# A list scheduler for everything behind the attention in an attention and two-expert-layer kernel

## The chip, the cores and the metric

The kernel runs on one core of a Trainium2 chip. The metric is the time of one execution on the device in microseconds (us); lower is better. A core has TensorE (PE: matmuls; PEld: its weight loads), VectorE (DVE), ScalarE (ACT) and GpSimd (POOL); SP issues most DMA. Each engine works through a queue of its own, in the order in which the program was written, and waits on semaphores for the others.

## The reference

```python
q_bits = (einsum('bhsd,dk->bhsk', q, proj) > 0)          # the same for k; 6 bits make a bucket
mask = q_bucket[..., :, None] == k_bucket[..., None, :]
attn = softmax(where(mask, q @ k.T / 8, -1e9)) @ v       # q, k, v: (2, 8, 768, 64)
x = attn.transpose(0, 2, 1, 3).reshape(1536, 512)
h = maximum(maximum(x @ w1, x @ w2), x @ w3)             # 512 -> 768
x = h @ w_out                                            # 768 -> 512
h = x @ w_in                                             # 512 -> 2048
g = where(h >= 1, h, where(h <= -1, 0, (h + 1) ** 2 / 4))
out = g @ w_out2                                         # 2048 -> 512
```

q, k, v and proj come as 32-bit floats, the layers' weights as 64-bit ones; the output is 32-bit.

## The kernel before

The attention works through the 16 heads (functions in `attention`); its order on every engine comes from an older planner, `Work`, and is the same in both kernels. It ends with the normalisation of the last pair of heads: `pair_recip`, the fold of two halves (L576, L580), a broadcast of the reciprocals by DMA (`rb<-d`, L605), `norm_mult` (L614), `norm_hi` and `norm_lo` (L623, L627). The first matmuls of the first expert layer are written in among these (the generator `mlp_steps`).

Everything behind it is `mlp`. Tokens lie in three tiles of 512 columns (`tok(c)`); every matrix product is made from three matmuls of a high and a low part (`mm3`, L308). Four products follow each other: the first layer (18 weights, the maximum of three kept in `h`), the second (`b<-hh`, 8 weights of 384 columns), the third with the activation `g` (`l3`, `g_out`), and the fourth, which adds into `acc` (`l4`, L1235, L1242). From the fifth weight of the first layer on, and in the third, weights are taken in pairs: `pair_units` makes four blocks of output from seven block products in place of eight. It needs four sums of the pair's weights (`s`, from `sr`, L245 to L250), three difference tiles of the input (`x_d`, from `raw`, L1027, L1104, L1020, L1023) and, on the way, copies of one PSUM bank into another, which seed it: among them the sum `d` (L1072), which VectorE writes from the bank `b` and `x7`. The next product into `b`, `product(b, "s1", T1, False)`, can't start before VectorE has read it. A pair is eleven units of six matmuls.

A weight is read as 64-bit words (`wr`), and has a front of one ScalarE and four VectorE steps (L211, L213, L218, L222, L226), which make a 32-bit value (`wg`), and a back of a ScalarE cast (L234, the high part) and a GpSimd subtraction (L268, the low part). Two tiles of raw words and seven of finished weights exist.

What sets the order is the program text: `w_tick(2)` after each unit takes the weights' work on by two steps, whichever weight is next; `flush` writes the split of the last result one result later; banks go around in the order in which they come free in the text. There are no costs and no due times behind the attention.

Of the kernel before, what the change touches and what calls it, by code (L numbers as in the profile page):

```python
# [111 lines left out]

@with_exitstack
def lsh_attention_moe_kernel(
# [85 lines left out]
    def w_steps(n):  # L200
# [11 lines left out]
        yield  # L212
# [3 lines left out]
        yield  # L216
        g2 = w_p.tile([128, 512], I32, tag="wg2", name="wg2", bufs=2)[:, 0:cols]
# [3 lines left out]
        yield  # L221
# [3 lines left out]
        yield  # L225
# [3 lines left out]
        yield  # L229
        if n % WBUFS < WEARLY:  # L230
            w = w_p.tile([128, 2, 512], F32R, tag="w", name="w", bufs=WEARLY)
        else:
            w = w_state["more"].tile([128, 2, 512], F32R, tag="wx", name="wx", bufs=WBUFS - WEARLY)
        nc.scalar.copy(out=w[:, 0, 0:cols], in_=f32(g2))  # L234
        splits[n] = w
        low_todo.append((n, w, g2, cols))
        g2s[n] = f32(g2)
        if n not in pair_at:
            return
        yield  # L240
        a1, a2 = g2s.pop(n - 1), g2s.pop(n)
# [1079 lines left out]
```

## Time and profile before

| | us |
|---|---|
| three timed runs | 673.18, 673.73, 677.01 |
| median | 673.73 |
| the profiled execution's own time | 671.09 |
| its span, first to last instruction | 669.3 |
| DVE busy in the span | 495.6 |
| ACT busy in the span | 396.6 |
| POOL busy in the span | 352.8 |

A share of busy time is a mean over stages with different limits; the rows below are therefore cut by stage. PE and DVE in the rows are TensorE and VectorE, L and a number is a line of the kernel, and `b<-x_hl,wx` reads: writes tile b, reads x_hl and wx. `PEclk` is the share of full clock that TensorE was granted (0.5 is 1.2 GHz, 1.0 is 2.4 GHz).

### The profile page before, as it was taken

What the parts mean: (1) busy time and instruction counts of PE and PEld (TensorE: products, weight loads), DVE (VectorE), ACT (ScalarE), POOL (GpSimd) and SP (SyncE); (2) the same over time, 40 slices, a digit from 0 to 9 for tenths busy, and PEclk for the clock granted to TensorE, in tenths of its full rate; (3) what the DMA queues carried; (4) which work ended last, traced back from release to release, by engine and by line L of the source; (5) the groups of instructions that cost most, each with busy time, mean ns of one, the idle gap of its engine ahead of it and who ended that gap; (6) DMA issues with size and microseconds to landing.
All of it is one profiled execution on the core that took longest, in us unless ns stands there. A gap on an engine that the chain in (4) does not pass through costs nothing.

```text
span 669.3 us, 11587 instructions
## 1 busy us (share of the span) xinstructions
PE 645.2 (96%) x4323; PEld 513.4 (77%) x4323; DVE 495.6 (74%) x803; ACT 396.6 (59%) x740; POOL 352.8 (53%) x313
## 2 busy tenths in 40 slices
PE   7999999999999899889999998799999999999998
PEld 5668777778867677768888886588888888888886
DVE  5788989999863899878844477655786969696554
ACT  7687877887782344555443246778748374646440
POOL 6437547766322577657645255754646464645340
PEclk8999999999999989999999999899999999999999
DMA  6857787786333012231211211221211212121004
GB/s 189 224 122 185 198 213 182 199 247 153 92 112 81 32 64 95 94 95 55 71 49 47 64 63 59 68 94 64 64 63 64 89 37 94 36 92 63 1 0 189
DMA packets 27857, 66.99 MB, mean 100 GB/s; under 512 B 4165, under 2 KB 9125, under 8 KB 27801
## 3 DMA queue, kind: packets, MB, share of 16 engines
q1 hardware_dynamic: 27488, 66.21, 33.9%
q8 instruction: 34, 0.56, 0.3%
q14 instruction: 23, 0.18, 0.1%
q10 hardware_dynamic: 312, 0.04, 0.0%
HBM read 46.17 MB, written 3.19 MB: 74 GB/s over the span
## 4 chain that ended last, share of the span: by engine, by line
PE 79%; DVE 12%; ACT 4%; issue 3%; DMA 1%; POOL 1%; DVEq 0%; ACTq 0%; SPq 0%; POOLq 0%
PE b L308 24%; PE b L1235 18%; PE u_ps L308 7%; PE s_ps L449 6%; PE t_ps L482 5%; PE u_ps L543 5%; PE s_ps L452 5%; PE u_ps L510 3%; DVE raw L1027 2%; PE u_ps L1235 2%; PE pj_ps L425 2%; DVE pj_ps L213 1%; DVE wg L226 1%; DVE wg L218 1%; DVE pj_ps L222 1%
## 5 line engine op out<-in xcount | busy, mean ns | idle before, releaser
L459 DVE TENSOR_SCALAR_CACHE_REDUCE p<-s_ps 128x768 f32<-128x768 f32 x96 | 89.7, 951 | 13.3 <-PE s_ps L452 10.0
L474 ACT ACTIVATE p<-p,nm 128x768 f32<-128x768 f32 x96 | 89.7, 936 | 7.2 <-DVE p L459 6.7
L1213 POOL TENSOR_TENSOR g<-r,g 128x512 fp32r<-128x512 f32 x48 | 62.7, 1306 | 37.9 <-ACT g L1212 37.7
L449 PE MATMUL s_ps<-lo,q 128*128 128x384 f32 x192 | 72.5, 378 | 3.1 <-POOL lo L416 2.0
L308 PE MATMUL b<-x_d,s 128*128 128x512 f32 x270 | 68.6, 398 | 6.4 <-DVE u_ps L1072 2.6
L1235 PE MATMUL b<-wx,g 128*128 128x512 f32 x264 | 67.5, 393 | 4.5 <-ACT wx L234 3.3
L308 PE MATMUL b<-x_hl,wx 128*128 128x512 f32 x264 | 65.7, 393 | 1.5 <-ACT x_hl L1163 1.2
L308 PEld LDWEIGHTS b<-x_d,s 128*128 128x128 f32 x270 | 51.2, 192 | 19.6 <-DVE u_ps L1072 3.4
L452 PE MATMUL s_ps<-hi,q 76*128 76x384 f32 x192 | 66.1, 344 | 0.0
L213 DVE SCALAR_TENSOR_TENSOR pj_ps<-pj_ps,wr 128x512 f32<-128x512 f32 (+1 forms) x55 | 37.2, 677 | 37.5 <-ACT pj_ps L211 37.5
L1235 PE MATMUL b<-w,g 128*128 128x512 f32 (+1 forms) x264 | 64.6, 384 | 0.0
L234 ACT CAST wx<-wg 128x512 fp32r<-128x512 f32 (+1 forms) x32 | 19.4, 605 | 73.3 <-DVE wg L226 73.3
L1235 PEld LDWEIGHTS b<-wx,g 128*128 128x128 f32 x264 | 49.8, 189 | 15.7 <-ACT wx L234 3.7
L268 POOL TENSOR_TENSOR wx<-wg,wx 128x512 fp32r<-128x512 f32 (+1 forms) x32 | 40.7, 1273 | 39.3 <-ACT wx L234 36.1
L308 PEld LDWEIGHTS b<-x_hl,wx 128*128 128x128 f32 x264 | 50.1, 190 | 12.7 <-ACT x_hl L1163 1.7
L308 PE MATMUL b<-x_hl,w 128*128 128x512 f32 (+1 forms) x282 | 59.5, 363 | 0.0
L1242 DVE TENSOR_TENSOR acc<-b,acc 128x512 f32<-128x512 f32 (+1 forms) x77 | 51.6, 677 | 8.9 <-PE b L1235 8.9
L1235 PEld LDWEIGHTS b<-w,g 128*128 128x128 f32 x264 | 48.9, 188 | 9.9
L308 PEld LDWEIGHTS b<-x_hl,w 128*128 128x128 f32 x282 | 48.0, 189 | 8.8 <-issue 0.6
L449 PEld LDWEIGHTS s_ps<-lo,q 128*128 128x128 f32 x192 | 36.7, 191 | 21.3 <-DVE p L459 8.6
L492 ACT COPY pt<-t_ps 128x768 f32<-128x768 f32 (+1 forms) x59 | 41.0, 706 | 17.0 <-PE t_ps L482 14.7
L268 POOL TENSOR_TENSOR w<-wg,w 128x512 fp32r<-128x512 f32 (+1 forms) x26 | 33.0, 1269 | 29.9 <-ACT w L234 26.8
(154 smaller groups left out, 1495.9 us busy)
## 6 DMA issues: line engine op xcount, KB each, us to landing
wr<-in_w SPq DMA_DIRECT2D x48, 512.0 KB
r<-in_kq SPq DMA_DIRECT2D x15, 384.0 KB
q<-hi SPq DMA_DIRECT2D x15, 384.0 KB
v<-in_v SPq DMA_DIRECT2D x21, 256.0 KB
rb<-d SPq DMA_DIRECT2D x16, 192.0 KB
wr<-in_w SPq DMA_DIRECT2D x8, 384.0 KB
q<-lo SPq DMA_DIRECT2D x15, 192.0 KB
lo<-hi SPq DMA_DIRECT2D x15, 192.0 KB
```

Source lines behind the costliest of these rows:

```text
L213: nc.vector.scalar_tensor_tensor(out=f32(g), in0=f32(g), scalar=TINY_SQ, in1=f32(high), op0=ALU.is_ge, op1=ALU.mult)
L268: nc.gpsimd.tensor_tensor(out=w[:, 1, 0:cols], in0=f32(g2), in1=f32(w[:, 0, 0:cols]), op=ALU.subtract)
L308: nc.tensor.matmul(out=outp, lhsT=w_[a], rhs=x_[b_], start=(begins and i == 0 and jj == 0), stop=(ends and i == n - 1 and jj == 2), skip_g ...
L449: nc.tensor.matmul(out=o, lhsT=hd["qa"][:, qs], rhs=hd["lo"][:, ks], start=True, stop=False)
L452: nc.tensor.matmul(out=o, lhsT=hd["qb"][0:76, qs], rhs=hd["hi"][0:76, ks], start=False, stop=True)
L459: nc.vector.tensor_scalar(out=p.rearrange("p (a k) -> p a k", a=2), in0=s_ps[bank.at][:, :, 0:HALF], scalar1=MASKED, scalar2=MASKED, op0=A ...
L474: nc.scalar.activation(out=p, in_=p, func=ACTF.Exp, scale=-1.0, bias=tl[n]["nm"], accum_out=sums_of(h // 2)[:, c:c + 1],)
L482: nc.tensor.transpose(out=t_ps[:, half, j * 128:(j + 1) * 128], in_=tl[n]["p"][:, kt * 128:(kt + 1) * 128], identity=ident,)
L492: copy(out=grp[g][:, 3 * a:3 * b_, r * 128:(r + 1) * 128].rearrange("p (a j) q -> p a j q", a=b_ - a), in_=t_ps[:, a:b_, 0:HALF].rearrange ...
L1213: nc.gpsimd.tensor_tensor(out=lo, in0=r, in1=f32(hi), op=ALU.subtract)
L1235: nc.tensor.matmul(out=pb[:, cs], lhsT=gs[f][:, a, tsl], rhs=wt[:, b_, cs], start=(n == 0), stop=(n == len(terms) - 1),)
L1242: nc.vector.tensor_tensor(out=acc[:, t, cs], in0=pb[:, cs], in1=acc[:, t, cs], op=ALU.add)
```

## The change

All work behind the attention is first noted as tasks of a new `Plan` (`add`: engine, cost in us, what it reads and writes), and written at the end by `plan.run()`. `dues` gives TensorE's tasks due times by its own line of products, in the order of the text, and works the other engines' due times back from them. `run` then takes, engine by engine, among the tasks that could start nearly at once the one that is due first. Buffers (`Pool`, `Buf`) are handed out one by one as tasks start. The costs are numbers in the source.

Besides the order, some of the work is cut otherwise:

- The steps of a weight are split into `w_front` and `w_back`. The fronts of weights 3 and 4 are written into the end of the attention, ahead of the fold and ahead of `norm_mult`.
- The first layer's difference tiles (`chain_of`) are made in halves of 512 columns: ScalarE copies the high part of x into a PSUM bank, and VectorE works on the bank. Before, seven VectorE and some GpSimd steps of 1024 columns in SBUF did it (`steps`, `add`, `less`, `cut`).
- Sums of weights are four tiles of 256 columns, each with a cast and a subtraction of its own, in place of two of 512.
- In the second layer the token tiles come in another order in three of four column blocks, and the difference tiles of the third layer are made from the banks directly.
- `h` and `r` share four buffers, `wg2` has three in place of two.

TensorE's matmuls are the same in number.

```diff
+class Plan:
+
+
+
+
+    HOP, NEXT, OVER, DRAIN = 0.06, 0.03, 0.09, 0.17
+    PATIENCE = dict(PE=0.1, ACT=0.15, DVE=0.15, POOL=0.3, SP=0.3)
...
+    def dues(self):
+        pe = self.at["PE"]
+        for t in self.tasks:
+            t["next"], t["wait"] = [], len(t["after"])
+            if t["eng"] == "PE":
+                t["due"] = pe
+                pe += t["cost"]
+            else:
...
+        for again in range(2):
+            for t in reversed(self.tasks):
+                if t["eng"] != "PE":
+                    nexts = t["next"] + [b.after for b in t["uses"] if b.at is None and b.after and b.after["n"] > t["n"]]
+                    t["due"] = min([x["due"] for x in nexts], default=pe) - t["cost"] - t["lag"] - self.HOP
+            for p in pools:
+                line = p.given if p.ordered else sorted(p.given, key=lambda b: (b.first["due"], b.turn))
...
+    def start_of(self, t):
+        eng = t["eng"]
+        x = self.at.get(eng, 0.0) - (self.OVER if eng in ("ACT", "DVE", "POOL") else 0.0)
+        for a in t["after"]:
+            x = max(x, a["end"] + self.NEXT * (eng != "PE") if a["eng"] == eng else a["done"] + self.HOP)
+        if t["lock"] or eng == "POOL":
+            x = max(x, self.lock)
+        for b in t["takes"]:
+            p = b.pool
+            if p.ordered and p.taken != b.turn:
+                return None
+            free = [f for f in p.free if not b.seeded or f[1] in self.whole]
+            if not free:
+                return None
+            x = max(x, min(free)[0] + self.HOP)
+        return x
...
+            for eng, ts in ready.items():
+                can = [(x, t) for t in ts if (x := self.start_of(t)) is not None]
+                if can:
+                    first = min(x for x, _ in can)
+                    x, t = min(((x, t) for x, t in can if x <= first + self.PATIENCE[eng]), key=lambda c: (c[1]["due"], c[1]["n"]))
+                    if best is None or x < best[0]:
+                        best = (x, t)
...
+        g2s[n] = f32(g2)
+
+    def w_back(n):
+        w = w_p.tile([128, 2, 512], F32R, tag=f"w{n}", name="w", bufs=1)
+        g2 = g2s.pop(n)
+        nc.scalar.copy(out=w[:, 0], in_=g2)
+        splits[n] = w
+        low_todo.append((n, w, g2))
+
+    def w_low():
+        for _, w, g2 in low_todo:
+            nc.gpsimd.tensor_tensor(out=w[:, 1], in0=g2, in1=f32(w[:, 0]), op=ALU.subtract)
+        low_todo.clear()
...
             pair_recip(last)
+            for _ in w_front(WEARLY):
+                pass
+            w_load(WEARLY + 2, nc.scalar)
             ahead_mm(2, 4)
             ahead_copy()
...
             for _ in range(2):
                 next(mlp_steps)
+            for _ in w_front(WEARLY + 1):
+                pass
             for half in range(2):
                 norm_mult(last, half, nc.vector)
                 norm_hi(last, half, nc.scalar.copy)
...
+            banks_ = Pool(7, bank_at, [(max(0.0, 0.55 * k - 0.35), n) for k, n in enumerate([6, *banks])], False)
+            turn_ = Pool(3, lambda n: None)
+            h_ = Pool(4, h_at, [2, 3])
+            s_ = Pool(8, s_at)
+            sr_ = Pool(4, lambda n: sr_p.tile([128, 256], F32, tag=f"sr{n}", name="sr", bufs=1))
...
+            wr_ = Pool(2, lambda n: w_p.tile([128, 512, 2], I32, tag=f"wr{n}", name="wr", bufs=1), [0])
+            g2_ = Pool(3, lambda n: w_p.tile([128, 512], I32, tag=f"wg2{n}", name="wg2", bufs=1), [2])
+            w_ = Pool(7, lambda n: (w_p if n < 3 else wx_p).tile([128, 2, 512], F32R, tag=f"w{n}", name="w", bufs=1), range(3, 7))
...
+                two(whole_(r3), half(a1, 0), half(a2, 0), ALU.subtract, [a1, a2], [r3], 0.42)
+                two(whole_(r2), half(a2, 1), whole_(r3), ALU.subtract, [a2, r3], [r2], 0.42)
+                cut_s("s3", r3)
+                cut_s("s2", r2)
+                two(whole_(r1), half(a2, 0), half(a2, 1), ALU.add, [a2], [r1], 0.42)
+                two(whole_(r4), half(a1, 1), whole_(r2), ALU.subtract, [a1, r2], [r4], 0.42)
+                cut_s("s1", r1)
+                cut_s("s4", r4)
...
+            def advance(base, pairs):
+                while True:
+                    n = state["back"]
+                    m = state["sums"]
+                    waits = m < len(PAIRS) and key_index[PAIRS[m][1]] < n
+                    if waits and m < pairs:
+                        sums(m)
+                        state["sums"] += 1
+                    elif n < min(base + 7, NSL) and not (waits and n > key_index[PAIRS[m][1]] + 1):
+                        while state["front"] <= n:
+                            front(state["front"])
+                            state["front"] += 1
+                        back(n)
+                        state["back"] += 1
+                    else:
+                        return
...
+            def chain_of(i):
+                of = lambda b: (lambda: b.t)
+
+                def whole_of(kk, c, o=None, key=None):
+                    b = buf(banks_, full=None, also=buf(turn_))
+                    hi, lo = (lambda: f32(x_hl[:, 0, kk, tok(c)])), (lambda: f32(x_hl[:, 1, kk, tok(c)]))
+                    copy(of(b), hi, [("x", kk, c, 0)], [b], 0.58)
+                    two(o or of(b), of(b), lo, ALU.add, [b, ("x", kk, c, 1)], [key or b], lock=False)
+                    return b
+
+                r, t2, t4 = (low_buf(m, i) for m in (0, 1, 3))
+                rl, t2l, t4l = (low_ap(x) for x in (r, t2, t4))
+                b = whole_of(i, 1)
+                whole_of(2 + i, 1, t2l, t2)
+                b1 = whole_of(i, 0, rl, r)
+                less(of(b1), of(b), rl, [b, r, b1], [b1], lock=False)
+                less(of(b), t2l, of(b), [t2, b], [b], lock=False)
+                cut(2, i, of(b), b, True)
+                two(t2l, of(b), rl, ALU.add, [b, r], [t2], lock=False)
+                cut(1, i, t2l, t2)
+                cut(0, i, of(b1), b1, True)
+                b = whole_of(2 + i, 0)
+                less(t4l, of(b), t2l, [b, t2], [t4], lock=False)
...
+                for c in (2, 0, 1) if j < 2 else (1, 0, 2) if j < 3 else (1, 2, 0):
+                    b = buf(banks_)
...
+            plan.run()
+            yield
```

VectorE at the end of the attention, from the reciprocal on (`wg<-wg,wr` and the three steps behind it are a front; weight 2's ends just ahead of the rows). Before:

```order
L587 RECIPROCAL sums<-sums 128x12
L576 COPY uc<-u_ps 64x384
L580 TENSOR_TENSOR u<-u,uc 128x384 x2
L969 TENSOR_TENSOR h_2774<-b_2813,h_2774 128x512
L614 TENSOR_TENSOR xr<-u,rb 128x384 x2
L969 TENSOR_TENSOR h_2811<-b_2833,h_2811 128x256
L627 TENSOR_TENSOR x_hl<-xr,x_hl 128x384 x2
```

Now:

```order
L355 SCALAR_TENSOR_TENSOR wg<-wg,wr 128x512
L360 TENSOR_SCALAR wg_2773<-wg 128x512
L364 SCALAR_TENSOR_TENSOR wg<-wg,wg_2773 128x512
L368 SCALAR_TENSOR_TENSOR wg_2773<-wr,wg 128x512
L682 COPY uc<-u_ps 64x384
L686 TENSOR_TENSOR u<-u,uc 128x384 x2
L1065 TENSOR_TENSOR h<-b_2822,h 128x512
L355 SCALAR_TENSOR_TENSOR wg<-wg,wr 128x512
L360 TENSOR_SCALAR wg_2841<-wg 128x512
L364 SCALAR_TENSOR_TENSOR wg<-wg,wg_2841 128x512
L368 SCALAR_TENSOR_TENSOR wg_2841<-wr,wg 128x512
L720 TENSOR_TENSOR xr<-u,rb 128x384 x2
```

A front stands ahead of the fold (L682, L686) and a second one ahead of `norm_mult` (`xr<-u,rb`).

VectorE at the start of `mlp`, where the difference tiles are made. Before:

```order
L213 SCALAR_TENSOR_TENSOR pj_ps<-pj_ps,wr 128x512
L1104 TENSOR_TENSOR raw<-x_hl 128x1024
L218 TENSOR_SCALAR wg_2945<-pj_ps 128x512
L222 SCALAR_TENSOR_TENSOR pj_ps<-pj_ps,wg_2945 128x512
L1104 TENSOR_TENSOR raw<-x_hl 128x1024
L1027 TENSOR_TENSOR raw<-raw 128x1024 x2
L969 TENSOR_TENSOR h_2811<-b_2813,h_2811 128x256
L226 SCALAR_TENSOR_TENSOR wg_2945<-wr,pj_ps 128x512
L1027 TENSOR_TENSOR raw<-raw 128x1024
L1023 TENSOR_TENSOR x_d<-raw,x_d 128x1024
```

Now:

```order
L1130 TENSOR_TENSOR b_2938<-b_2938,x_hl 128x512
L1130 TENSOR_TENSOR s<-b_2851,x_hl 128x512
L1130 TENSOR_TENSOR s<-b_2807,x_hl 128x512
L1130 TENSOR_TENSOR b_2851<-b_2938,s 128x512
L1130 TENSOR_TENSOR b_2938<-s,b_2938 128x512
L1130 TENSOR_TENSOR s<-b_2938,s 128x512
L1130 TENSOR_TENSOR h<-b_2867,h 128x256
L1130 TENSOR_TENSOR x_d<-b_2938,x_d 128x512
L1130 TENSOR_TENSOR u_ps<-u_ps,x_hl 128x512
L1130 TENSOR_TENSOR s<-u_ps,s 128x512
L1130 TENSOR_TENSOR h<-b_2881,h 128x512
L1130 TENSOR_TENSOR b_2807<-b_2807,x_hl 128x512
```

The steps of 1024 columns are gone, one input of each new step is a bank (`b`, `u_ps`), and the fronts (`pj_ps`) have moved behind them.

VectorE at the change from the second layer to the third and fourth. `wg_4422` before and `wg_4385` now is the second weight of the fourth product. Before:

```order
L213 SCALAR_TENSOR_TENSOR pj_ps<-pj_ps,wr 128x512
L218 TENSOR_SCALAR wg_4383<-pj_ps 128x512
L222 SCALAR_TENSOR_TENSOR pj_ps<-pj_ps,wg_4383 128x512
L226 SCALAR_TENSOR_TENSOR wg_4383<-wr,pj_ps 128x512
L1203 SCALAR_TENSOR_TENSOR r<-r,b_2833 128x512
L213 SCALAR_TENSOR_TENSOR pj_ps<-pj_ps,wr 128x512
L218 TENSOR_SCALAR wg_4422<-pj_ps 128x512
L1203 SCALAR_TENSOR_TENSOR r<-r,b_2813 128x512
L1203 SCALAR_TENSOR_TENSOR r<-r,y 128x512
L222 SCALAR_TENSOR_TENSOR pj_ps<-pj_ps,wg_4422 128x512
L226 SCALAR_TENSOR_TENSOR wg_4422<-wr,pj_ps 128x512
L1203 SCALAR_TENSOR_TENSOR r<-r,b_2908 128x512
```

Now:

```order
L1130 TENSOR_TENSOR s<-b_2938,s 128x512
L1130 TENSOR_TENSOR h<-b_2938,s 128x512
L1130 TENSOR_TENSOR x_hl<-b_2938,x_hl 128x512
L1170 SCALAR_TENSOR_TENSOR wg_4385<-wr,pj_ps 128x512
L1161 SCALAR_TENSOR_TENSOR pj_ps<-pj_ps,wr 128x512
L1164 TENSOR_SCALAR wg_4442<-pj_ps 128x512
L1130 TENSOR_TENSOR x_hl<-b_2881,x_hl 128x512
L1130 TENSOR_TENSOR sr<-wg_4188,sr 128x256
L1167 SCALAR_TENSOR_TENSOR pj_ps<-pj_ps,wg_4442 128x512
L1170 SCALAR_TENSOR_TENSOR wg_4442<-wr,pj_ps 128x512
L1130 TENSOR_TENSOR h<-b_2822,h 128x512
L1130 TENSOR_TENSOR x_hl<-b_2822,x_hl 128x512
```

Its last step (L226, now L1170) stood behind results of the third layer (`r<-r`); now it stands ahead of the last split of the second layer (`x_hl<-b`).

## Rows read from the trace of the kernel before

**Rows 1.** the page, busy time, share of the span and instructions of each engine:
```profile
PE 645.2 (96%) x4323; PEld 513.4 (77%) x4323; DVE 495.6 (74%) x803; ACT 396.6 (59%) x740; POOL 352.8 (53%) x313
```

**Rows 2.** windows: us, busy us (x) of PE, PEld, DVE, ACT, POOL; PEclk, DMA share, GB/s:
```profile
207.43:230.03 22.60, 22.60 (x134) 19.80 (x132) 15.14 (x18) 3.85 (x8) 7.98 (x3) 1.00 0.16 46
230.03:291.22 61.19, 52.41 (x212) 40.88 (x211) 54.01 (x77) 31.14 (x54) 41.93 (x29) 0.94 0.26 86
291.22:405.60 114.38, 114.38 (x505) 94.70 (x505) 74.30 (x114) 52.01 (x97) 55.80 (x45) 1.00 0.20 63
405.60:434.80 29.20, 22.57 (x91) 17.11 (x90) 20.83 (x32) 21.04 (x38) 21.68 (x17) 0.93 0.18 62
434.80:438.77 3.97, 3.97 (x14) 3.15 (x12) 1.41 (x3) 3.59 (x7) 1.90 (x2) 0.67 0.42 132
438.77:663.35 224.58, 224.58 (x992) 185.97 (x991) 159.51 (x253) 126.84 (x223) 111.91 (x87) 1.00 0.19 64
```

**Rows 3.** timeline of PE, 225 to 300: start, us, instruction, idle before and releaser:
```profile
231.89 0.73 PE L308 MATMUL u_ps<-x_hl,wx 128*128 128x512 f32 x2 [1.86 <-ACT wx L234]
233.51 4.63 PE L308 MATMUL u_ps<-x_hl,wx 128*128 128x512 f32 x10 [0.89 <-POOL wx L268]
...
273.72 1.66 PE L308 MATMUL b<-x_d,s 128*128 128x512 f32 x6 [1.88 <-DVE b L1072]
...
291.22 1.66 PE L308 MATMUL b<-x_d,s 128*128 128x512 f32 x6 [2.24 <-DVE u_ps L1072]
```

**Rows 4.** timeline of PE, 376 to 440:
```profile
410.39 0.50 PE L308 MATMUL b<-x_hl,wx 128*128 128x512 f32 x1 [1.23 <-ACT x_hl L1163]
...
431.72 0.80 PE L1235 MATMUL b<-wx,g 128*128 128x512 f32 x1 [3.27 <-ACT wx L234]
433.78 1.22 PE L1235 MATMUL b<-wx,g 128*128 128x512 f32 x2 [1.27 <-POOL wx L268]
```

**Rows 5.** groups by line and shape of DVE, 209.3 to 291.22: count, busy us, mean ns:
```profile
L1027 DVE TENSOR_TENSOR raw<-raw 128x1024 f32<-128x1024 f32 x4 | 9.0, 2255 | 0.0
...
L969 DVE TENSOR_TENSOR h<-b,h 128x512 f32<-128x512 f32 x11 | 7.5, 684 | 0.1
L226 DVE SCALAR_TENSOR_TENSOR wg<-wr,pj_ps 128x512 int32<-128x512 int32 x10 | 6.8, 684 | 0.2
...
L247 DVE TENSOR_TENSOR sr<-wg,sr 128x256 f32<-128x256 f32 x4 | 3.6, 912 | 0.1
L1104 DVE TENSOR_TENSOR raw<-x_hl 128x1024 f32<-128x1024 f32 x2 | 3.4, 1690 | 0.0
...
L1023 DVE TENSOR_TENSOR x_d<-raw,x_d 128x1024 fp32r<-128x1024 f32 x1 | 1.7, 1725 | 0.5 <-ACT x_d L1020 0.5
...
L969 DVE TENSOR_TENSOR h<-b,h 128x256 f32<-128x256 f32 x4 | 1.7, 418 | 0.6 <-PE b L308 0.6
```

**Rows 6.** timelines of DVE and of SP's queue at the end of the attention:
```profile
209.37 0.56 DVE L576 COPY uc<-u_ps 64x384 f32<-64x384 f32 x1 [8.12 <-ACT u L575]
...
214.02 1.03 DVE L614 TENSOR_TENSOR xr<-u,rb 128x384 f32<-128x384 f32 x2 [1.29 <-DMA rb<-d]
...
215.30 1.02 DVE L627 TENSOR_TENSOR x_hl<-xr,x_hl 128x384 fp32r<-128x384 f32 x2
...
231.10 1.22 DVE L1027 TENSOR_TENSOR raw<-raw 128x1024 f32<-128x1024 f32 x1
...
209.38 1.11 SPq L605 DMA_DIRECT2D rb<-d  x2
210.53 87.53 SPq L196 DMA_DIRECT2D wr<-in_w  x13
```

**Rows 7.** timelines of DVE, ACT and POOL, steps on the second output weight:
```profile
430.32 0.69 DVE L226 SCALAR_TENSOR_TENSOR wg<-wr,pj_ps 128x512 int32<-128x512 int32 x1
...
431.06 0.61 ACT L234 CAST wx<-wg 128x512 fp32r<-128x512 f32 x1
...
432.46 1.27 POOL L268 TENSOR_TENSOR wx<-wg,wx 128x512 fp32r<-128x512 f32 x1
```

More of the change, by code (lines that the diff above doesn't have):

```diff
@@ L110, in run, with __init__ @@
         assert not left, left
+class Pool:
+    def __init__(self, slots, make, free=None, ordered=True):
+        self.slots, self.make, self.ordered = slots, make, ordered
+        self.free = [x if isinstance(x, tuple) else (0.0, x) for x in (range(slots) if free is None else free)]
+        self.taken, self.given = 0, []
+class Buf:
+    def __init__(self, pool, seeded=False, full=True, at=None, tile=None, also=None):
+        self.pool, self.seeded, self.full, self.at, self.t, self.also = pool, seeded, full, at, tile, also
+        self.users, self.end, self.first = 0, 0.0, None
@@ L228, in w_steps @@
         )
-        yield
[L230 to L241, printed above, removed]
@@ L934, in mlp, with tok, bank_at @@
             ps = mx.enter_context(tc.tile_pool(name="ps_m", bufs=1, space=PSUM, reuse_waits="tile"))
[L935 to L940 removed]
+            banks, whole, at_bank, seen = list(range(6)), set(), {6: u_ps}, {}
+            def tok(c):
+                return slice(c * TCH, (c + 1) * TCH)
+            def bank_at(n):
@@ new lines, in mlp @@
+            first = slice(0, S - TCH)
+            for i, (w, c) in enumerate((w, c) for w in range(3) for c in range(2) if w or c):
+                cs = first if c else slice(0, TCH)
+                n = banks.pop(0)
+                pb = bank_at(n)[:, cs]
+                l1_mm(w_get(("1", 0, w)), pb, slice(c * TCH + cs.start, c * TCH + cs.stop))
+                l1_out(pb, 0, c, cs, hraw.get((0, c)))
+                banks.append(n)
+                if c == 0:
+                    whole.add(n)
+                else:
+                    whole.discard(n)
@@ new lines, in xk, with wk2, unit @@
+            def xk(kk, c):
+                return [("x", kk, c, p) for p in range(2)]
+            def wk2(w):
+                return [(w, 0), (w, 1)]
+            def unit(b, left, right, begins, ends, rd, seeded=False, cost=MM):
+                pairs = len(left())if False else None
+                n = sum(1 for _ in rd)
+                return add("PE", cost, lambda: mm3(b.t, list(zip(left(), right())), begins, ends, seeded), rd if begins else [*rd, b], [b], chain="PE")
+            h_of = {(0, c): buf(h_, at=c, tile=hraw[0, c]) for c in range(2)}
```

738 lines of the change are left out of this document (416 added, 322 removed).

## The prediction

> **What bounds the kernel now.** I first read how busy TensorE is over the span, then cut its span into stages, then looked for who ends its waits in the stages that have any. Over the span it is busy 96% [rows 1], which looks finished; the stages say otherwise [rows 2]. From 291.22 to 405.60 and from 438.77 to 663.35 it never waits: 114.38 us of 114.38 and 224.58 of 224.58, at full clock. By the source they hold 504 and 990 matmuls of 512 columns, 0.2269 and 0.2268 us each; I use 0.2268. Nothing that another engine does there is worth anything. What is left is two stretches.
>
> The first is the start of the expert layers, 230.03 to 291.22. The source has 210 matmuls there (36 of the fourth first-layer weight, two pairs of 66, and 42 of the third): 210 x 0.2268 = 47.6 us in 61.2, so **13.6 us** are lost. 8.8 are waits (61.19 - 52.41), the rest a clock of 0.94 and restarts [rows 2]. TensorE waits at 231.89 for a weight that ScalarE casts after VectorE, then at half clock takes 4.63 us for ten matmuls, and at 273.72 and 291.22 waits 1.88 and 2.24 us for VectorE's sum that seeds the next bank [rows 3]. VectorE is busy 54.0 of these 61.2 us [rows 2]: it is what paces the stretch.
>
> The second is where the second expert block begins, 405.60 to 434.80: 90 matmuls, 20.4 us in 29.2, so 8.8 lost, and 12 more at clock 0.67 until 438.77 take 3.97 in place of 2.72, 1.25 more [rows 2]: **10.05 us**. The waits are 1.23 us for a tile of the layer before, then 3.27 and 1.27 for the second output weight [rows 4]. VectorE is only 71% busy here (20.83 of 29.20). Its last step on that weight ends at 431.0 and GpSimd's low half at 433.7 [rows 7]: the work is late by its place in the queues, not by its size.
>
> So the change can give at most 13.6 + 10.05 = 23.6 us on the profiled execution, whose own time is 671.09.
>
> **The change part by part.** TensorE has the same 1872 wide and 84 narrow matmuls after the attention in both kernels, in nearly the same order: only the bank that each fills differs, and the order of the token tiles in three of the four column blocks of the second layer. Attention is untouched up to its last reciprocal.
>
> *Two weight fronts moved into the tail.* VectorE is idle 8.12 us before 209.37 [rows 6]. The front of weight 3 (four VectorE steps of 0.69, 2.8 us, [rows 5]) now stands there; its raw words have been loaded since long before. It ends near 208, so it costs nothing, and the wait at 230 goes. The front of weight 4 stands ahead of the last head's normalisation, and there it is not free. Its load moves ahead of the row broadcast on the SP queue, where it stood behind it (210.53 against 209.38, [rows 6]); the four steps add 2.8 us ahead of the normalisation, whose low half ended at 216.3 (215.30 + 1.02, [rows 6]). That makes 219.1. Queued behind it on VectorE are the maxima of the first layer; waiting for it on TensorE is the fourth slice of the tile after the first 36 narrow and 24 wide matmuls from 207.43. A narrow one takes 0.125 (22.60 us less 60 wide ones, over 72, [rows 2]), so that tile starts at 217.4 and wants the slice nine matmuls on, at 218.5. Bounds: 0 if the two loads land together as now, 2.5 if the broadcast, now waited for until 214.02 [rows 6], lands 1.9 later. I take 0.5, nearer the first, since both orders move the same bytes.
>
> *The difference tiles of the first layer.* Seven VectorE steps on 1024 columns become twenty on 512, with ScalarE copying into PSUM banks that are free then, so that one input of each is in PSUM. The seven took 9.0 + 3.4 + 1.7 = 14.1 us [rows 5], 1.7 to 2.3 each by the groups, though one in which GpSimd was idle took 1.22 [rows 6]. A 512-column step with one input in PSUM takes 0.68 [rows 5], twenty make 13.8. VectorE's bill is equal; GpSimd loses its two large additions, ScalarE gains eight copies and has the room. The Trainium skill speaks against this part: Perfetto Trace Analysis, Optimizing Scalar/DVE Operations, says that each VectorE instruction pays a fixed access overhead and that grouping into larger operations helps when the engine is saturated, as it is here. By that rule splitting the seven makes the bill longer, and the sum below would keep some 5 us more; the means just given say that six of the seven came nowhere near their shortest, so I take the rows, and keep that outcome as a rival.
>
> *Order by due time at the start.* What decides is when the first pair's third sum is ready, since its product T1 is the tightest. TensorE, unhindered, reaches it after 36 + 42 = 78 matmuls: 230.03 + 17.7 = 247.7. By the new order VectorE has 52 instructions from 209.37 up to that sum: 13 front steps (9.0), 9 maxima (5 of 0.68, 4 of 0.42: 5.1), the 20 above (13.8), 3 sums (0.42 to 0.91, 2.2), and 7 of the tail at about 0.55 (3.9): 34.0 us, 243.4. Add 2 to 4 us of waits (the fold's and the broadcast's loads, ScalarE's copies into banks), then ScalarE and GpSimd on a quarter tile, about 1.0 (an estimate: half of the 0.61 and 1.27 that a 512-column tile takes, [rows 7]): 246.5 to 248.5. The wait is 0 to 2 there; I take 1.5 for GpSimd's interference. By the third pair's T1 (277.6, where the kernel before arrives at 291.22) the same sum, 82 instructions (29 front steps, 14 maxima, the 20, 10 sums at 0.75, 2 seeds, 7 of the tail), is 55.7 us, 265.1: VectorE is then some 10 us ahead, so the seeds at 273.72 and 291.22 are not late again. With 0.5 for restarts the stretch keeps 2.5 of its 13.6; bounds 0 and 8.
>
> *Order by due time at the second block.* The front of the second output weight now ends ahead of the last second-layer split, so some 4 us before the second block starts instead of 25 after (431.0 - 405.6); it is needed 19 us after. The tile that the 1.23 us wait is for comes one block (18 matmuls, 4.1 us) earlier. What is late next: the last split of g that the fourth product's first tile reads, whose product ends 12.4 us after the start (54 matmuls and the drain); five ScalarE steps of some 0.65 and GpSimd's 1.3 are queued before it is whole, 17 us, against 19. I keep 1 of 10.05, bounds 0 and 4.5.
>
> *Steady stretches.* Sums in four 256-column pieces rather than two of 512 add two ScalarE and two GpSimd instructions per pair, under 1 us of 15. VectorE is busy 159.5 of 224.6 there [rows 2], so the added work lies beside TensorE. New order may still put a step just in time; I allow 1, bounds 0 and 5.
>
> Sum: 671.1 - 23.6 + 2.5 + 1 + 1 = 652.0 in a profiled execution. The three runs shown lie 2.1 to 5.9 above the profiled one, their median 2.6; I add 2: **654 us**.
>
> **Rivals.** *Half recovered:* VectorE stays saturated at the start, since twenty steps of 0.69 replace seven that could take 1.22, 8.5 in all, were GpSimd quiet: 5.3 more, all on the path at T1, and the second stretch keeps its 4.5 too. That gives 654 + 5.3 + 3.5 = 663. Against it: the seven took 14.1, and GpSimd is not quiet there. The grouping rule of the Trainium skill quoted above would have it so. *The planner's costs miss:* waits arise elsewhere for each removed, 20 us come back, about 672; the order speaks against it, as fronts do move ahead of need. *Slower:* "as late as due" makes the seed sum late in every pair. There are 15 pairs after the start; the two late seeds now cost 1.88 and 2.24 [rows 3], 2.06 x 15 = 31 us, 654 + 31 = 685. It decides above 19.6 / 15 = 1.3 us a pair. For it: the seed stands behind fronts in VectorE's queue in both kernels. Against it: in the steady rows VectorE has 65 us to spare, so a step that is ready is seldom held back.
>
> **How the numbers follow.** The forecast (648 to 659) gets 0.76, half recovered (659 to 664) 0.12, no change 0.07, slower 0.04, under 648 0.01. The range 648 to 663 takes the first and most of the second. A run of this kernel can tell 1% (6.7 us) from no change: faster by over that 0.89, within 0.07, slower 0.04.
>
> **What would show it.** No wait near 230 and clock 1.00 from there on; the third pair's T1 near 280 instead of 291.22; the first matmul of the output layer without a wait for a cast; VectorE still over 85% busy from 221 to 250, at 0.69 a step; a wait of 0 to 2.5 near 218 and one near 248. Wrong if VectorE's 512-column steps take over 1 us beside GpSimd, if the broadcast lands after 216, or if gaps of over 1 us recur once a pair.

## The result, and the profile after

The changed kernel takes **649.98 us** (median of 4 runs, 646.67 to 651.22) against 674.05 for the kernel before (4 runs, 673.18 to 677.01): a ratio of **0.9628**, 95% interval 0.958 to 0.9676. The forecast was 654, its range 648 to 663. The profiled run took 649.12 us, its span is 647.0 (before: 671.09 and 669.3).

First the page of the changed kernel: the busy line and, of the 40 slices, the granted clock. They answer to [rows 1].

```profile
PE 637.9 (99%) x4323; PEld 510.0 (79%) x4323; DVE 485.7 (75%) x818; ACT 404.6 (63%) x778; POOL 341.8 (53%) x340
PEclk9999999999999999999999999999999999999999
```

Then the windows by stage, cut at the same matmuls as in [rows 2]: the narrow tiles; the start of the expert layers up to the third pair's T1; the rest of the first layer and the second; the second block's first 102 matmuls; and the steady rest.

```profile
core 0: us, PE busy (x) PEld busy (x) DVE busy (x) ACT busy (x) POOL busy (x), PEclk, DMA share, GB/s
207.03:230.40 23.37, 22.86 (x134) 20.05 (x133) 17.96 (x33) 10.77 (x22) 5.22 (x5) 1.00 0.29 90
230.40:278.39 47.99, 47.99 (x213) 39.41 (x211) 41.87 (x69) 28.20 (x57) 33.35 (x33) 1.00 0.23 77
278.39:393.38 114.99, 114.54 (x506) 94.55 (x505) 84.39 (x142) 59.98 (x119) 67.86 (x64) 1.00 0.26 83
393.38:416.47 23.09, 23.09 (x103) 19.15 (x102) 16.13 (x26) 21.06 (x39) 15.25 (x13) 1.00 0.28 92
416.47:641.05 224.58, 224.58 (x992) 186.02 (x991) 151.56 (x237) 125.94 (x228) 109.63 (x96) 1.00 0.17 57
```

The start went from 61.19 to 47.99 us, the second block from 33.17 to 23.09; TensorE is busy for all of both, at full clock. VectorE stays as full there as it was: it is busy 41.87 of 47.99 us (87%; before 54.0 of 61.2, 88%). But it does 12.1 us less in the stretch: eight weight fronts in place of ten (2.8 us each), weight sums of 8.2 us in place of 11.9, and fewer maxima and steps of the difference tiles, more of which now fall ahead of it (17.96 against 15.14). Behind the stretch it is busier, 84.39 us against 74.30, and TensorE has hardly a wait there. So the new order also puts off work that TensorE does not need yet. Since the clock and the waits are one account, I read all kernels below by one number: from the first narrow matmul to TensorE's last, the **expert part**. It was 207.43 to 666.14, 458.7 us; it is 207.03 to 643.84, **436.8**. Without any loss the matmuls take 1872 x 0.2268 + 84 x 0.125 = 435.1. So 21.9 of the 22.3 us of span come from here, and 1.7 are left. A second profile of the same kernel (e9) has an expert part of 434.75 us, so a difference of 2 us or less between two profiles is not taken for one below.

From the first narrow matmul on, TensorE's timeline of the changed kernel has three waits (in brackets: idle time before the row, and who ended it). The other rows stand where the kernel before waited in [rows 3] and [rows 4] or where the forecast has a wait: the 96 matmuls from 219.40 run past 230 without a wait, 248.18 is the first pair's T1, 278.39 the third pair's T1, and 412.42 the first output matmul.

```profile
218.34 0.38 PE L414 MATMUL u_ps<-x_hl,w 128*128 128x256 f32 x1 [0.17 <-ACT x_hl L729]
219.06 0.50 PE L414 MATMUL u_ps<-x_hl,w 128*128 128x256 f32 x2 [0.34 <-DVE x_hl L733]
219.40 19.43 PE L414 MATMUL b<-x_hl,w 128*128 128x512 f32 x96
...
248.18 1.52 PE L414 MATMUL b<-x_d,s 128*128 128x512 f32 x6
...
278.39 1.52 PE L414 MATMUL b<-x_d,s 128*128 128x512 f32 x6
...
308.92 1.66 PE L414 MATMUL b<-x_d,s 128*128 128x512 f32 x6 [0.45 <-DVE b L1130]
...
412.42 1.52 PE L1503 MATMUL b<-w,g 128*128 128x512 f32 x6
```

VectorE's groups by shape from 218 to 252 in the changed kernel: fronts, difference tiles and sums. They answer to [rows 5].

```profile
L1161 DVE SCALAR_TENSOR_TENSOR pj_ps<-pj_ps,wr 128x512 f32<-128x512 f32 x4 | 2.8, 695 | 1.0 <-ACT pj_ps L1160 1.0
...
L1130 DVE TENSOR_TENSOR sr<-wg,sr 128x256 f32<-128x256 f32 x3 | 2.2, 740 | 0.0
...
L1130 DVE TENSOR_TENSOR s<-b,s 128x512 f32<-128x512 f32 x3 | 2.1, 691 | 0.4 <-ACT x_d L1127 0.3
L1130 DVE TENSOR_TENSOR b<-b,x_hl 128x512 f32<-128x512 f32 x3 | 2.1, 689 | 0.0
L1130 DVE TENSOR_TENSOR x_d<-b,x_d 128x512 fp32r<-128x512 f32 x3 | 2.0, 683 | 0.3 <-ACT x_d L1127 0.3
...
L1130 DVE TENSOR_TENSOR sr<-wg 128x256 f32<-128x256 f32 x1 | 1.2, 1234 | 0.0
```

The twenty steps of the difference tiles are eleven such groups, all between 678 and 699 ns: 13.8 us. The sums, which read and write SBUF alone, spread from 0.41 to 1.39: in the group `sr<-wg,sr` two steps of 0.41 stand beside one of 1.39.

### The profile page after: what moved, and what is told of

Same layout as the page of the kernel before. It is cut to its first block, busy times and chain, and to the rows that moved or that the text cites. A ratio compares the mean times of both kernels' runs of the same rounds, so it can differ in the third digit from the quotient of the medians.

```text
span 647.0 us, 11690 instructions
## 1 busy us (share of the span) xinstructions
PE 637.9 (99%) x4323; PEld 510.0 (79%) x4323; DVE 485.7 (75%) x818; ACT 404.6 (63%) x778; POOL 341.8 (53%) x340
## 4 chain that ended last, share of the span: by engine, by line
PE 92%; DMA 3%; DVE 2%; ACT 1%; issue 1%; POOL 0%; SPq 0%; DVEq 0%; ACTq 0%; POOLq 0%
PE b L414 39%; PE b L1503 17%; PE u_ps L414 6%; PE s_ps L555 6%; PE t_ps L588 5%; PE u_ps L649 5%; PE s_ps L558 5%; PE u_ps L1503 4%; PE u_ps L616 3%; PE pj_ps L531 2%; PE t_ps L616 1%; DMA wr<-in_w 1%; DMA uc<-u 1%; DMA rb<-d 1%; PE pj_ps L616 0%
## 5 line engine op out<-in xcount | busy, mean ns | idle before, releaser
L414 PE MATMUL b<-x_hl,w 128*128 128x512 f32 (+1 forms) x702 | 161.6, 380 | 0.0
L414 PEld LDWEIGHTS b<-x_hl,w 128*128 128x128 f32 x702 | 127.7, 188 | 25.7 <-issue 0.6
L1503 PE MATMUL b<-w,g 128*128 128x512 f32 (+1 forms) x480 | 113.7, 386 | 0.0
L1136 POOL TENSOR_TENSOR w<-wg,w 128x512 fp32r<-128x512 f32 (+1 forms) x55 | 69.7, 1272 | 72.1 <-ACT w L1127 71.9
L1503 PEld LDWEIGHTS b<-w,g 128*128 128x128 f32 x480 | 89.4, 188 | 18.3
L1136 POOL TENSOR_TENSOR g<-h,g 128x512 fp32r<-128x512 f32 x48 | 61.8, 1295 | 72.4 <-ACT g L1127 72.4
L1130 DVE TENSOR_TENSOR acc<-b,acc 128x512 f32<-128x512 f32 (+1 forms) x70 | 47.6, 680 | 25.6 <-PE b L1503 25.5
L1136 POOL TENSOR_TENSOR s<-sr,s 128x256 fp32r<-128x256 f32 x60 | 44.3, 753 | 19.7 <-ACT s L1194 17.8
L598 ACT COPY pt<-t_ps 128x768 f32<-128x768 f32 (+1 forms) x59 | 41.0, 706 | 16.6 <-PE t_ps L588 14.1
L588 PE MATMUL t_ps<-ident,p 128*128 128x128 f32 x324 | 45.0, 275 | 1.3 <-ACT pt L598 1.1
L605 DVE STREAM_TRANSPOSE dt<-p 128x768 f32<-128x768 f32 x42 | 40.1, 968 | 8.1 <-PE pj_ps L616 7.5
L588 PEld LDWEIGHTS t_ps<-ident,p 128*128 128x128 f32 x324 | 37.2, 141 | 10.6 <-ACT p L580 4.3
```

Source lines behind the costliest of these rows:

```text
L414: nc.tensor.matmul(out=outp, lhsT=w_[a], rhs=x_[b_], start=(begins and i == 0 and jj == 0), stop=(ends and i == n - 1 and jj == 2), skip_g ...
L588: nc.tensor.transpose(out=t_ps[:, half, j * 128:(j + 1) * 128], in_=tl[n]["p"][:, kt * 128:(kt + 1) * 128], identity=ident,)
L598: copy(out=grp[g][:, 3 * a:3 * b_, r * 128:(r + 1) * 128].rearrange("p (a j) q -> p a j q", a=b_ - a), in_=t_ps[:, a:b_, 0:HALF].rearrange ...
L605: nc.vector.transpose(out=dt[:, DT_AT[h] + t], in_=tl[n]["p"].rearrange("p (b k) -> p b k", k=32))
L1130: return add("DVE", cost, lambda: vector.tensor_tensor(out=out_(), in0=a(), in1=b_(), op=op), rd, wr, lock)
L1136: return add("POOL", cost, lambda: pool_.tensor_tensor(out=out_(), in0=a(), in1=b_(), op=op), rd, wr)
```

## The experiments

Ten runs were made, on three chips. Times are medians, ratios are to the kernel before on the same chip; TensorE's expert part is read from each profile. The attention, the same program in all variants of the changed kernel but for the fronts in its tail, ends between 206.07 and 210.70 in these profiles, so spans differ by that too.

**e1: no due times.**

```
-  key=lambda c: (c[1]["due"], c[1]["n"])
+  key=lambda c: c[1]["n"]
```

> The changed kernel, but of the steps that could start soonest on an engine the scheduler takes the one that was recorded first, not the one that is due first. Theory (the due times are what brings the gain): two weight fronts stand ahead of the difference tiles again, 5.6 us of VectorE work, the first pair's third sum (ready near 246.7 in the changed kernel, wanted at 248.2) is some 4 us late, and fronts and seed sums collide later too: 655 to 670 us. Rival (cutting the work into short steps, with more buffers and fronts in the tail, is enough, any sensible order does): within 2 us of the changed kernel, 648 to 652, with no wait of over 1 us on TensorE near 248.

Measured: **659.72 us**, ratio 0.9792 (0.977 to 0.9815); expert part 446.5. The size fits the theory, its mechanism does not. TensorE's only long wait is not at T1:

```profile
217.39 11.27 PE L414 MATMUL b<-x_hl,w 128*128 128x512 f32 x60
237.91 4.58 PE L414 MATMUL b<-x_hl,w 128*128 128x512 f32 x12 [9.25 <-DVE x_d L1130]
```

The matmul at 237.91 starts a new tile: it reads no difference tile, and is released by the VectorE step that frees a bank of one (it starts at 237.16 and ends at 237.85). VectorE's timeline of the same run shows where the banks were: four maxima, each of which empties a bank, stand in one row behind all difference tiles, the first sums and one more front.

```profile
237.16 0.69 DVE L1130 TENSOR_TENSOR x_d<-b,x_d 128x512 fp32r<-128x512 f32 x1 [0.65 <-ACT x_d L1127]
...
243.57 1.94 DVE L1130 TENSOR_TENSOR h<-b,h 128x256 f32<-128x256 f32 x4
```

One wait of 0.37 follows at 287.74, and after 290 this kernel waits nowhere. So the due times matter only at the start, where VectorE is full; in the second block and the steady stretches the same scheduler without them loses nothing. They are worth 9.7 of the 21.9 us; the other 12.2 come without them, from the rest of the change: the order in which the tasks are noted, the shorter steps, the fronts in the tail and the additional buffers. What the smaller weight sums and the buffers add by themselves no run shows.

**e5: a rule in place of the due times.** e1 with the first layer's maxima taken before anything else that could start:

```
-  key=lambda c: c[1]["n"]
+  key=lambda c: ("out" not in c[1], c[1]["n"])
...
-  two(..., ALU.max, [b, h], [h], 0.69 * f, not psum)
+  two(..., ALU.max, [b, h], [h], 0.69 * f, not psum)["out"] = 1
```

Its expectation names the copies out of the banks too; the mark was put on the maxima alone.

> The kernel without due times (e1), with one rule in their place: of the steps that could start, VectorE and ScalarE take the first layer's maxima and copies out of the banks first, then the one recorded first. Theory (what the due times did at the start was to set the maxima among the difference tiles, so that TensorE has a bank): the wait of 9.25 us goes, the first pair's third sum is up to 4 us late for the two fronts ahead of the tiles: 650 to 655 us. Rival (the fronts ahead of the tiles cost it, banks or not): a wait of 4 us or more remains before 260, 657 to 661.

Measured: **653.91 us**, ratio 0.9701 (0.9663 to 0.974); expert part 439.3. The wait for a bank is gone, and 7.2 of e1's 9.7 us with it. What is left is mostly what I had expected of e1 as a whole, the first pair's weight sums, late behind the two fronts, though at its first sums and not at the third; the last row waits for a seed:

```profile
245.22 0.73 PE L414 MATMUL b<-x_d,s 128*128 128x512 f32 x2 [1.16 <-ACT s L1194]
246.89 2.56 PE L414 MATMUL b<-x_d,s 128*128 128x512 f32 x10 [0.94 <-POOL s L1136]
283.71 1.66 PE L414 MATMUL b<-x_d,s 128*128 128x512 f32 x6 [1.31 <-DVE b L1130]
```

**e2: difference tiles from SBUF to SBUF.** The copies into banks go, the intermediate tiles stand in two SBUF tiles that are idle then; twenty VectorE steps of 512 columns as in the changed kernel. With the copies goes `lock=False`: the scheduler now tries to keep these steps apart from GpSimd's, so that part of what e2 costs may lie in another order.

```
 def whole_of(kk, c, o=None, key=None, pool=x7_):
-    b = buf(banks_, full=None, also=buf(turn_))
-    copy(of(b), hi, [("x", kk, c, 0)], [b], 0.58)
-    two(o or of(b), of(b), lo, ALU.add, ...)
+    b = None if key else buf(pool)
+    two(o or of(b), hi, lo, ALU.add, ...)
...
-    b1 = whole_of(i, 0, rl, r)
+    whole_of(i, 0, rl, r)
+    b1 = buf(y_)
```

> The changed kernel, but the difference tiles are made from SBUF to SBUF: no ScalarE copies into PSUM banks, the same VectorE steps of 512 columns. Theory (a PSUM operand is what keeps these steps at 0.69 us beside GpSimd): their mean goes to 1.0 to 1.4 us, sixteen to twenty of them make 5 to 14 us, the third sum has 1.5 us to spare, so TensorE waits 4 to 12 us at the first pair's T1: 654 to 662 us. Rival (what is gained is the order alone; the steps are no slower from SBUF, and eight ScalarE copies fewer): 648 to 652, steps of 0.7 us.

Measured: **653.14 us**, ratio 0.9691 (0.9668 to 0.9714); expert part 440.5. VectorE's groups by shape, 218 to 252:

```profile
L1130 DVE TENSOR_TENSOR x<-x_hl 128x512 f32<-128x512 f32 x4 | 3.9, 974 | 0.0
L1130 DVE TENSOR_TENSOR s<-x_hl 128x512 f32<-128x512 f32 x4 | 3.7, 955 | 0.0
L1130 DVE TENSOR_TENSOR s<-x,s 128x512 f32<-128x512 f32 x4 | 3.2, 808 | 0.1
...
L1130 DVE TENSOR_TENSOR x_d<-y,x_d 128x512 fp32r<-128x512 f32 x2 | 2.4, 1224 | 0.0
...
L1130 DVE TENSOR_TENSOR x_d<-x,x_d 128x512 fp32r<-128x512 f32 x2 | 1.6, 810 | 0.0
...
L1130 DVE TENSOR_TENSOR x<-s,x 128x512 f32<-128x512 f32 x2 | 1.4, 686 | 0.0
L1130 DVE TENSOR_TENSOR y<-x,s 128x512 f32<-128x512 f32 x2 | 1.4, 678 | 0.0
```

These twenty make 17.6 us, a mean of 0.88, where the changed kernel's make 13.8 at 0.69. Of the theory the direction holds, and no more: the mean is under its 1.0 to 1.4, the time lies between its range and the rival's, and the place is another. The third sum is not late (its VectorE step ends at 244.15, its low half at 245.94). T1 waits, in the first pair and in the second, until VectorE has read its bank for the seed:

```profile
248.94 1.66 PE L414 MATMUL u_ps<-x_d,s 128*128 128x512 f32 x6 [0.89 <-DVE b L1130]
...
265.66 1.66 PE L414 MATMUL b<-x_d,s 128*128 128x512 f32 x6 [1.45 <-DVE b L1130]
```

With three more (0.35, 0.24 and, at 406.52, 1.05) the waits are 3.98 us. The mean hides two kinds: steps of 0.68 to 0.75 and steps of 0.94 to 1.79. Rows of VectorE, and under them rows of GpSimd, show what sorts them: where both run, the one that starts second is the long one.

```profile
226.13 0.69 DVE L1130 TENSOR_TENSOR s<-x,s 128x512 f32<-128x512 f32 x1
...
232.36 0.70 DVE L1161 SCALAR_TENSOR_TENSOR pj_ps<-pj_ps,wr 128x512 f32<-128x512 f32 x1
...
233.64 1.77 DVE L1130 TENSOR_TENSOR x_d<-y,x_d 128x512 fp32r<-128x512 f32 x1
235.34 0.68 DVE L1130 TENSOR_TENSOR x<-x_hl 128x512 f32<-128x512 f32 x1
...
240.34 1.79 DVE L1130 TENSOR_TENSOR x<-x_hl 128x512 f32<-128x512 f32 x1
```

```profile
226.22 1.76 POOL L1136 TENSOR_TENSOR w<-wg,w 128x512 fp32r<-128x512 f32 x1 [4.01 <-ACT w L1127]
...
231.87 1.30 POOL L1136 TENSOR_TENSOR w<-wg,w 128x512 fp32r<-128x512 f32 x1 [0.91 <-ACT w L1127]
233.12 1.74 POOL L1136 TENSOR_TENSOR hh<-h,hh 128x512 fp32r<-128x512 f32 x1
...
240.28 1.29 POOL L1136 TENSOR_TENSOR x_d<-s,x_d 128x512 fp32r<-128x512 f32 x1 [5.42 <-ACT x_d L1127]
```

The VectorE steps at 233.64 and 240.34 start behind a GpSimd step, end 0.55 and 0.56 us after it, and take 1.77 and 1.79. The step at 226.13 starts ahead of one and keeps its 0.69; there it is the GpSimd step that takes 1.76 in place of 1.30. The front step at 232.36, with one operand in PSUM, took 0.70 though it started under a GpSimd step, which kept its 1.30. The planner knew the rule (these steps carry its lock), and keeping them apart is not always possible. The Trainium skill has a rule for this: Perfetto Trace Analysis, Optimizing Scalar/DVE Operations, says that GpSimd and VectorE share an SBUF read port, and that a VectorE operation on two ports holds it as an exclusive lock. The trace agrees, if a step with two SBUF operands counts as one, and puts the price at up to 1.1 us for a VectorE step and some 0.45 for a GpSimd step.

**e3 and e6: the fronts of the tail.** e3 leaves both out of the tail, and with them the early load of weight 5 (`w_load`); e6 leaves out the second front (WEARLY + 1) alone. The scheduler places what is left out.

```
 pair_recip(last)
-for _ in w_front(WEARLY):
-    pass
-w_load(WEARLY + 2, nc.scalar)
...
-for _ in w_front(WEARLY + 1):
-    pass
```

> The changed kernel without the two weight fronts in the tail of the attention; the scheduler places them after it. Theory (VectorE's sum up to the first pair's third sum decides, and it has some 1.5 us to spare): the tail ends 2.8 us sooner on VectorE, 5.6 us of fronts come after it, the third sum is 2.5 to 3 us later, TensorE waits 1 to 2.5 us at the first pair's T1 and nowhere for a weight: 650 to 653 us. Rival (the tail fronts carry the gain at the start, the weight is late again at 230 and the clock falls behind it): 656 us or more.

> The changed kernel with the front of weight 3 alone in the tail; the scheduler places that of weight 4. Theory (VectorE's work up to the third sum is the same, only its order differs): the waits of 0.17 and 0.34 near 218 go, the front comes back after the normalisation, the wait at the first pair's T1 stays under 1: within 1.5 us of the changed kernel, 648.5 to 651.5. Rival (the second tail front fills time in which VectorE only waits for the broadcast, so without it 2.8 us are added to a saturated engine): TensorE waits 1 to 2.8 at T1, 651 to 653.

Measured: e3 **651.82 us**, ratio 0.9667 (0.9641 to 0.9694), expert part 438.1; e6 **648.65 us**, ratio 0.9617 (0.9587 to 0.9646), expert part 434.8. e3's waits are small and spread, none for a weight at 230:

```profile
246.37 2.56 PE L414 MATMUL b<-x_d,s 128*128 128x512 f32 x10 [0.15 <-POOL s L1131]
...
263.26 2.01 PE L414 MATMUL u_ps<-x_d,s 128*128 128x512 f32 x6 [0.57 <-ACT s L1189]
```

A third, at 407.76, is of 1.04 for a seed sum. The wait of 1 to 2.5 us at the first pair's T1 did not come; the two waits of the start are 0.72 us together. By the ratios, 0.9667 against 0.9628 and 0.9637 (e9), the tail's fronts are worth 2 to 3 us, with intervals that overlap, and are not what carries the start; the theory's range was met, by way of other waits than its own. In e6 TensorE waits nowhere: VectorE lies idle 2.63 us for the row broadcast, in which the second front stood, but the sum still comes out in time. The second front in the tail is worth nothing that can be measured, as e9 and e10 bear out.

**e9 and e10: is e6 better than the changed kernel?** Both again, on one chip.

> The changed kernel itself, timed beside the next run on one chip, so that a difference of 1 us between the two can be read: 648 to 651 us, a wait of 0 to 0.6 us near 218 and one of 0.45 near 309.

> The version of e6 (only the front of weight 3 in the tail), timed beside the changed kernel. If the second tail front costs what the rows of e6 say (0.5 us at 218, 0.45 at 309 and the clock behind them, 436.8 us of expert layers against 434.8): 1 to 2 us under the run beside it. Rival (that difference is the spread of single profiles): within 0.7 us of it.

Measured: e9 **648.77 us**, ratio 0.9637 (0.9623 to 0.965); e10 **648.11**, ratio 0.9635 (0.9617 to 0.9653). No difference, as the rival said. The changed kernel's own second profile has no wait and an expert part of 434.75 us, e10's 434.76: the waits near 218 and at 308.92 come and go from one profile to the next. The attention ended at 207.03 in the first and at 210.51 in the second; that this is the reason is not shown. No version that beats the changed kernel measurably was found, and with these matmuls nothing is left to gain in the expert part: 434.75 us is what they take without a loss (435.1 by the sum above).

**e4: the second output weight, late again.** Its front may start only behind the second matmul group of the block's second pair.

```
+  held = ["hold"] if n == 31 else []
-  func=ACTF.Square), [r], [p])
+  func=ACTF.Square), [r, *held], [p])
...
+  [b, "hold"] if (m, n, i) == (L1P + 1, 0, 0) else [b]
```

> The changed kernel, but the front of the second output weight may start only 78 matmuls into the second expert block, about where the kernel before had it; the weight is whole some 4 us after the first output matmul wants it. Theory (the second block's loss came from that weight's place in the queues, and a wait there costs a lower clock behind it as well): a wait of 3 to 4 us and a granted clock under 0.8 for some 4 us, 5 to 9 us in all: 655 to 659 us. Rival (the wait alone costs): 3 to 4 us, 653 to 654. If the loss of the second block had another cause: under 2 us.

Measured: **655.71 us**, ratio 0.9715 (0.9681 to 0.9749); expert part 442.8.

```profile
413.39 0.84 PE L1505 MATMUL b<-w,g 128*128 128x512 f32 x3
416.59 0.49 PE L1505 MATMUL b<-w,g 128*128 128x512 f32 x1 [2.36 <-ACT w L1127]
418.27 1.22 PE L1505 MATMUL b<-w,g 128*128 128x512 f32 x2 [1.19 <-POOL w L1136]
419.29 5.32 PE L414 MATMUL b<-x_d,s 128*128 128x512 f32 x12
424.41 1.59 PE L1505 MATMUL b<-w,g 128*128 128x512 f32 x6
```

```profile
413.00:420.00 7.00, 3.45 (x11) 2.32 (x10) 6.75 (x10) 5.53 (x10) 5.90 (x5) 0.83 0.21 75
420.00:424.00 4.00, 4.00 (x11) 3.02 (x11) 1.39 (x2) 1.78 (x4) 1.99 (x2) 0.50 0.39 131
```

The rows of [rows 4] are back: the same two waits for the same two releasers, 2.36 and 1.19 us, and then a granted clock of 0.50 from 420 to 424. From 413.39 to 424.41 eighteen matmuls take 11.0 us in place of 18 x 0.2268 = 4.1: 6.9 lost, of which the waits are 3.6. A wait here costs twice its length.

**e7: the kernel before, with one front in the tail.** The first two lines stand in `w_tick`.

```
+if w_state["done"] >= WEARLY and not w_state["more"]:
+    return
...
 pair_recip(last)
+w_state["gen"] = w_steps(WEARLY)
+for _ in range(5):
+    next(w_state["gen"])
```

> The kernel before, with the four VectorE steps of weight 3's front moved into the tail of the attention, where VectorE is idle; nothing else changed. Theory (that wait at 231.89 is only where a saturated VectorE shows first): the waits of 1.86 and 0.89 go with the half clock behind them, but the later ones grow, since VectorE's bill falls by 2.8 us of some 54: 670 to 672 us against 674. Rival (the late weight and the clock that it costs are most of the stretch): 664 to 668.

Measured: **671.61 us**, ratio 0.9972 (0.9952 to 0.9992).

```profile
231.38 9.69 PE L310 MATMUL b<-x_hl,wx 128*128 128x512 f32 x42
243.50 0.73 PE L310 MATMUL b<-x_d,s 128*128 128x512 f32 x2 [2.42 <-ACT s L256]
246.79 2.07 PE L310 MATMUL b<-x_d,s 128*128 128x512 f32 x4 [2.56 <-POOL s L258]
```

The waits at 231.89 and 233.51 [rows 3], 2.75 us, are gone, and 4.98 us of new ones stand at the next thing that VectorE owes, the first pair's sums, with the granted clock at 0.50 behind them (249.6 to 252.6). The later waits for seeds, 1.88 and 2.24 us at the start before, did not grow as expected; the longest wait for VectorE's seeds is now 0.72. Taking one late item off a full engine moved the wait: the expert part stayed where it was (458.2 us against 458.7). The medians differ by 1.7 us (0.5 to 3.2 by the interval); of the profiled spans' 1.8 us, 1.2 lie in the attention, which ended at 206.23.

**e8: the token tiles of the second layer in the older order.**

```
-  for c in (2, 0, 1) if j < 2 else (1, 0, 2) if j < 3 else (1, 2, 0):
+  for c in (2, 0, 1) if j < 1 else (0, 1, 2) if j < 2 else (1, 0, 2):
```

> The changed kernel with the second layer's token tiles in the order of the kernel before, as far as its steps allow (0, 1, 2 in the second column block, 1, 0, 2 in the fourth). Theory (the tile that the second block waited 1.23 us for is now ready by its place in the order): a wait of 0.5 to 2 us on TensorE in the first twenty matmuls of the second expert block, 650.5 to 652. Rival (the scheduler's due times alone bring it in time): no wait there, 649 to 650.5.

Measured: **649.13 us**, ratio 0.9632 (0.9599 to 0.9664); no wait in the second block, one of 0.44 at 310.04. The rival holds: the scheduler needs no help from that order. In the first column block and in the two later ones the order could not be put back fully, since steps there read others' results.

## Why the prediction was right

The time lies 4.0 us under the forecast and inside its range; the mechanism that it forecast is in the main what the runs show: the waits at the start go because VectorE's work comes in another order (e1, e5), and those of the second block because its weight comes early (e4). What decides within that order the prediction had otherwise: not the third sum, but banks that have to be emptied (e1) and seeds that have to be read (e2). By its own terms:

- **The ceiling, 23.6 us.** The expert part gained 21.9, so 1.7 of it is left, in two waits near 218 (0.5), one at 308.92 (0.45) and slow restarts behind them. In e9 none of it is left.
- **The start, 2.5 kept of 13.6.** Kept: 47.99 - 47.6 = 0.4 behind 230.40, and 23.37 - 22.60 = 0.8 ahead of it, 1.2 in all. The 0.5 for the normalisation behind the second front came out exactly (0.17 + 0.34), but by luck: in e9, with the same front, there is no wait, and the working behind it was off in two places. The front itself waited 1.98 us for ScalarE's first step on its weight, and the broadcast does land later behind a weight's load, though both orders move the same bytes: VectorE had it 5.95 and 6.34 us after its issue in e6 and e10, where such a load stands just ahead, and 4.64 and 4.55 in the kernel before and e3, where none does. The 1.5 for the first pair's T1 was too much. I had VectorE's third sum 34.0 us and 2 to 4 of waits after the fold's first step; it ended 36.45 us after that step began, as the 52nd instruction, the number that I had counted (first row; the second is the seed):

```profile
244.10 1.23 DVE L1130 TENSOR_TENSOR sr<-wg 128x256 f32<-128x256 f32 x1
...
246.92 0.69 DVE L1130 TENSOR_TENSOR b<-b,x 128x512 f32<-128x512 f32 x1
```

  Two errors cancel in this: VectorE was busy 30.67 of the 36.45 us, since steps of 0.69 can start 0.60 apart and their durations add up to more than they take, and idle 5.8. The sum's low half was whole at 246.60, 1.6 us ahead of T1 at 248.18. Nor was it the tightest of what T1 needs: VectorE had read T1's bank for the seed only at 247.61, 0.6 us ahead, and when e2 made VectorE's steps longer T1 waited for that and not for the sum. Of the signs in the prediction, the wait near 248 did not come, and whether the broadcast landed after 216 can't be read: VectorE was at the second front until 217.27 and never waited for it.
- **Difference tiles, 13.8 against 14.1.** Measured 13.8. The reason was only half told: the sum took the price of a step with an operand in PSUM without saying what it depends on. e2 shows it: the same steps from SBUF cost 17.6. And one row was misread: GpSimd was not idle beside the step of 1.22 at 231.10. Its step on `wx` started at 231.91, second, and took 1.55.
- **The second block, 1 kept of 10.05.** Nothing was kept (23.09 us for 102 matmuls, 23.1 at full pitch). That the weight's place was the cause is shown by e4; that its price would be the waits and a slow clock behind them, too. The part on the token order was not needed, as far as e8 could put the old order back.
- **Steady stretches, 1.** 0.6 (114.99 against 114.38), and none from 416.47 on.
- **From profile to median, 2.** It was 0.9 (649.98 - 649.12), 1.1 less. With the 2.9 by which the profiled run came in under 652.0, that is the whole difference. The term is no more than spread: in e9 the profiled run lies 1.8 above the median.

Of the rivals, *half recovered* rested on the rule that grouped steps are cheaper. Nothing here tried 1024-column steps in the new order, so of the rule only this is shown: halving the steps cost nothing as long as one operand was in PSUM. *Slower*, the seed sum late in every pair, happened once, for 0.45 us, and in e9 not at all. *The planner's costs miss* did not occur; e1 shows how far a wrong order goes, 9.7 us, and what it would be: a bank not emptied in time, which no step of the prediction had named.

## What to carry to other kernels

When one engine paces a stretch, taking the latest item off it moves the wait to the next one (e7: 2.75 us of waits gone, 4.98 new ones). The whole queue has to be put in order of need, so that work which is not needed yet can go behind the stretch, and first of all come the steps that give a buffer back to the engine that is waited for (e5: 7.2 of 9.7 us). Where the engine had time to spare, the order in which the tasks were noted did as well as the due times (e1 after 290), but a weight that was late there cost about twice its waits (e4). Beside GpSimd, the VectorE steps here were cheaper with an operand in PSUM, even with a ScalarE copy to put it there (e2).

## What was not expected of the hardware

A VectorE step of 512 columns that reads two SBUF tiles took 0.68 us alone and up to 1.79 when a GpSimd step had started ahead of it; where it started first, it took 0.69 to 0.75 and the GpSimd step 1.74 to 1.76 in place of 1.30 (e2). With one operand in PSUM it took 0.68 to 0.70 in every case. The clock fell to 0.50 for some 4 us after two waits of 3.6 us in all (e4: 6.9 us lost) and to a mean of 0.59 around one of 9.25 (e1: 11.0 us lost, of which 9.25 are the wait and the rest the twelve matmuls behind it, 4.58 in place of 2.88), but stayed at 1.00 through the waits of 0.15 to 1.45 us of e2, e3 and e5, and through the single ones of 1.88 and 2.24 in the kernel before. So a wait does not always cost twice its length.
